# Two passes of one half instead of one pass of two, and a lighter VectorE queue while weights are converted

## The chip, the cores and the metric

The kernel runs on one core of one Trainium2 chip. A core has five engines that work side by side, each from its own queue in a fixed order: TensorE (PE in the profile, with its weight loads as PEld), VectorE (DVE), ScalarE (ACT), GpSimd (POOL) and SyncE (SP), which here issues the transfers. They wait for one another by semaphores. The metric is the device time of one execution in microseconds. The kernel before ran three times: 958.40, 961.85 and 962.46 us, median 961.85.

## The reference

Three blocks, one after the other, all in float32 (the weights of the second come as float64):

- **Attention.** 4 batches, 8 heads, 768 positions, head width 64. A position sees itself and the 127 before it, and the first 4 positions ("sinks"). `a = softmax(q k^T / 8 + mask)`, `out = a v`.
- **MoE.** The attention's output as 3072 tokens of 512 numbers: `y = (sigmoid(x Wg) * (x Wv)) Wo` with 1536 inner columns.
- **Soft MoE.** `logits = y phi` with 32 slots; a softmax over all tokens gathers slots, 8 experts of two layers each work on them, and a softmax over slots spreads the result back over the tokens.

## The kernel before

The tokens fall into 8 **halves** of 384 (batch x half of the sequence). Attention is done half by half: 4 head pairs, each in 3 **units** of 128 queries, so 12 units a half and 96 in all. MoE works on 12 **chunks** of 128 inner columns, each with three weight tiles of 128 x 512 (g, v, o), so 36 tiles. Each number is split into a high and a low part that TensorE multiplies apart (three products instead of one).

**A unit of attention.** `stage_a` multiplies queries and keys (L296), reads the scores out of PSUM with the mask added into `P` (L300, VectorE), and, as the mask leaves at most one of two overlapping key blocks alive in each column, merges the two blocks to 128 columns by a minimum (L306, VectorE); ScalarE takes the exponential of 4 sink columns and 128 others (L312), and one step later `norm` divides by the sum (L316 and L317 on VectorE, L318 on GpSimd). `stage_b` transposes the 128 columns on TensorE (L344) and takes the two key blocks apart again with a triangular mask, twice over 256 columns (L355, VectorE). `stage_c` multiplies by the values (L370).

**A tile of weights.** In its first use a tile comes as float64 bits. `w_start` issues ScalarE's absolute value of the high words (L480); then, one step per call of `w_advance`, `s1` clamps and shifts (L483, L484, VectorE), `s2` puts the sign back (L487) and scales the low words (L488), both VectorE, `s3` adds the two (L491, GpSimd), and `s4` writes the float32 tile to a scratch in DRAM and splits it: the high part on ScalarE (L190), the low part on GpSimd (L462). In every later pass over the weights a tile is loaded from the scratch and only split again (`w_parts`).

**Passes.** `passes` groups the halves: (0,1), (2,3), (4,5), (6,7). A pass goes once over all 12 chunks, and a split tile is used for both halves of the pass; there is room for four chunks of split tiles (`slot`), and a tile of chunk n waits until chunk n-4 is done with (`before`). A step of two chunks and one half is four `gemm1` operations (L595, with the gate's product on VectorE at L606, its high part on ScalarE at L190, later VectorE at L192, and its low part on GpSimd at L608) and three `gemm2` operations (L630, summed on VectorE at L635). The tables `w_due` and `due` say at which operation a tile or a half is needed; `LA` is how many operations ahead a tile may be started, and the loop spreads the attention's pieces up to the due times. Before that loop, a first one does the attention of half 0 alone. An L608 is done once per chunk and half, so 24 of them make a pass of two halves and 96 the MoE. The framework then lists the instructions of each engine in an order that it works out itself, so the order in the code isn't that of the queues.

Of the kernel before, what the change touches and what calls it, by code (L numbers as in the profile page):

```python
# [9 lines left out]
F32 = mybir.dt.float32  # L10
F32R = mybir.dt.float32r
I32 = mybir.dt.int32
BF16 = mybir.dt.bfloat16
U32 = mybir.dt.uint32
# [22 lines left out]
def fused_kernel(ctx, tc, qT, kA, kB, vB, vS, wg, wv, wo, phi, w1, w2, n_sink, window, out):  # L37
# [10 lines left out]
    def ps(tag, bufs, dt=F32):  # L48
        return psum.tile([128, 512], dt, name=tag, tag=tag, bufs=bufs)
# [224 lines left out]
    def stage_a(u):  # L274
        n, jj = units[u]
        hf, p = pairs[n]
        if jj == 0:
            b, s = divmod(hf, 2)
            if s == 0 and p == 0:
                sinks(b)  # L280
            VT[n] = at.tile([128, 4, 128], F32, name="vt", tag="vt", bufs=2)
            sp.dma_start(out=VT[n][:, 0:3 + s], in_=vB[b, p, :, 2 * s:3 + 3 * s])
            while any(t[0] == n for t in at_tasks):
                run_split()
            load_pair(n + 2)
            queue_split(n + 1)
            PC[n] = at.tile([128, 3, 2, 132], F32, name="PC", tag="PC", bufs=2)
        j = 3 * (hf % 2) + jj
        w0, w, mt, blks, sk = UNITS[j]
        P = at.tile([128, 2, 260], F32, name="P", tag="P", bufs=3)  # L290
        nb = at.tile([128, 2], F32, name="nb", tag="nb", bufs=4)
        sm = at.tile([128, 2], F32, name="sm", tag="sm", bufs=4)
        Ss = [ps("ys", 3) for h in range(2)]
        for i, k in enumerate(QK[n][1:]):
            for h in range(2):
                pe.matmul(Ss[h][:, 0:w], QK[n][0][h][:, 128 * jj:128 * jj + 128], k[h][:, w0:w0 + w],  # L296
                          start=(i == 0), stop=(i == len(QK[n]) - 2))
        for h in range(2):
            S = Ss[h]
            dve.tensor_tensor_reduce(  # L300
                out=P[:, h, 0:w], in0=S[:, 0:w], in1=mask[:, MOFF[mt]:MOFF[mt] + w], scale=-0.125,
                scalar=3.0e38, op0=ALU.add, op1=ALU.min, accum_out=nb[:, h:h + 1])

        if sk is not None:
            c0 = sk + 4 if sk else 4
            dve.tensor_tensor(P[:, :, c0:c0 + 128], P[:, :, blks[0][1]:blks[0][1] + 128],  # L306
                              P[:, :, blks[1][1]:blks[1][1] + 128], op=ALU.min)
            src, dst = P[:, :, sk:sk + 132], PC[n][:, jj]
        else:
            src, dst = P[:, :, 0:128], PC[n][:, jj, :, 4:132]  # L310
        for h in range(2):
            act.activation(out=dst[:, h], in_=src[:, h], func=ACTF.Exp, scale=-1.0,  # L312
                           bias=nb[:, h:h + 1], accum_out=sm[:, h:h + 1])

        def norm():
            dve.tensor_scalar(sm, sm, 1.0e-9, None, op0=ALU.add)  # L316
            dve.reciprocal(sm, sm)  # L317
            pool.tensor_tensor(dst, dst, sm.unsqueeze(2).to_broadcast([128, 2, src.shape[2]]), op=ALU.mult)  # L318
            normed.add(u)
            if jj == 2:  # L320
                later(1, sink_parts)

        def sink_parts():
            T, u0 = T2[n % 2], 1 - hf % 2
            cb = PC[n].rearrange("p u h c -> p (u h) c")[:, 2 * u0:6, 0:4]
            cb = cb.unsqueeze(2).to_broadcast([128, 6 - 2 * u0, 2, 4])
            hi, lo = (T[:, 2 * u0:6, :, i] for i in range(2))
            dve.tensor_copy(hi, cb)
            dve.tensor_tensor(lo, cb, hi.bitcast(F32), op=ALU.subtract)
            sunk.add(n)  # L330
        later(1, norm)

    PC, normed, sunk = {}, set(), set()

    def stage_b(u):
        n, jj = units[u]
        hf, p = pairs[n]
        j = 3 * (hf % 2) + jj
        sk = UNITS[j][4]
        while u not in normed or jj == 2 and n not in sunk:  # L340
            tick()
        pt = ps("pt", 1)
        for h in range(2):
            pe.transpose(pt[:, 128 * h:128 * h + 128], PC[n][:, jj, h, 4:132], ident)  # L344
        if jj == 2:
            T, tt = T2[n % 2], tt2[n % 2]
            pe.transpose(pt[:, 256:384].bitcast(F32R), T.rearrange("p u a x s -> p (u a x s)"), identr)
        pts = at.tile([128, 2, 2, 128], F32, name="pts", tag="pts", bufs=4)
        st[u] = pts
        pv = pt[:, 0:256].rearrange("p (h q) -> p h q", h=2)  # L350
        if sk is None:
            act.copy(pts[:, 0], pv)
        else:
            for i in range(2):
                dve.tensor_tensor(pts[:, i], pv, tri[:, i].unsqueeze(1).to_broadcast([128, 2, 128]), op=ALU.mult)  # L355
        if jj == 2:
            for i in range(1 - hf % 2, 3):
                act.copy(tt[32 * i:32 * i + 32, 128 * i:128 * i + 128], pt[32 * i:32 * i + 32, 256:384])

    def stage_c(n):  # L360

# [45 lines left out]
        return True  # L407


    passes = [[h, h + 1] for h in range(0, NH, 2)]  # L410
    W64 = wg.dtype == mybir.dt.int64
    dram = ctx.enter_context(tc.tile_pool(name="dram", bufs=1, space=bass.MemoryType.DRAM))
    wscr = {kd: dram.tile([NF, 128, 512], F32, name="ws" + kd) for kd in "gvo"} if W64 else None
# [53 lines left out]
    def w_start():  # L467
        n, kind = wtiles[ws_n[0]]
        r = w_raw.pop((n, kind))
        ws_n[0] += 1  # L470
        if not (n < NF and W64):
            w_parts(n, kind, r)
            w_load()
            return


        L, H = r[:, :, 0], r[:, :, 1]
        A = tops[0].tile([128, 512], I32, name="wA", tag="wA", bufs=3)
        S = tops[0].tile([128, 512], I32, name="wS", tag="wS", bufs=2)
        act.activation(out=A.bitcast(F32), in_=H.bitcast(F32), func=ACTF.Abs)  # L480

        def s1():
            dve.tensor_scalar(A.bitcast(F32), A.bitcast(F32), F64_LO, F64_HI, op0=ALU.max, op1=ALU.min)  # L483
            dve.tensor_scalar(A, A, 3, 0x3FFFFFF8, op0=ALU.logical_shift_left, op1=ALU.bitwise_and)  # L484

        def s2():
            dve.scalar_tensor_tensor(A, H, -0x40000000, A, op0=ALU.bitwise_and, op1=ALU.bitwise_or)  # L487
            dve.tensor_scalar(S, L.bitcast(U32), 2.0 ** -29, None, op0=ALU.mult)  # L488

        def s3():  # L490
            pool.tensor_tensor(A, A, S, op=ALU.add)  # L491
            w_load()

        def s4():
            sp.dma_start(out=wscr[kind][chunks[n]], in_=A.bitcast(F32))
            w_parts(n, kind, A.bitcast(F32))
        w_fly[n, kind] = deque([s1, s2, s3, s4])
# [15 lines left out]

    def w_slot():
        w_advance()
        if w_can(LA) and len(w_fly) < 3:
            w_start()

    xs = {}
# [455 lines left out]
    while done_half[0] < 1:  # L975
        attn_piece()
        tick()
        w_slot()
    while w_can(0) or w_fly:
        w_slot()  # L980
    fast = nc.values_load(flag, min_val=0, max_val=1)
    phase[0] = 0

# [114 lines left out]
```

## Time and profile before

| | |
|---|---|
| three runs | 958.40, 961.85, 962.46 us |
| the profiled execution | 956.84 us, its span 955.0 us |
| busy over the span | PE 903.7, PEld 739.1, DVE 650.8, POOL 477.5, ACT 351.0 us |
| last weight tile converted (36th L491) | ends at 270.2 us |
| 24th, 48th, 72nd and 96th L608 | end at 327.3, 524.6, 718.9 and 879.3 us |

Busy time is the time in which an engine works on instructions; a wait inside an instruction counts as busy. PEclk is TensorE's granted clock as a share of 2.4 GHz. The idle time of an engine that nothing waits for costs nothing, so the stretches have to be read one by one.

### The profile page before, as it was taken

What the parts mean: (1) busy time and instruction counts of PE and PEld (TensorE: products, weight loads), DVE (VectorE), ACT (ScalarE), POOL (GpSimd) and SP (SyncE); (2) the same over time, 40 slices, a digit from 0 to 9 for tenths busy, and PEclk for the clock granted to TensorE, in tenths of its full rate; (3) what the DMA queues carried; (4) which work ended last, traced back from release to release, by engine and by line L of the source; (5) the groups of instructions that cost most, each with busy time, mean ns of one, the idle gap of its engine ahead of it and who ended that gap; (6) DMA issues with size and microseconds to landing.
All of it is one profiled execution on the core that took longest, in us unless ns stands there. A gap on an engine that the chain in (4) does not pass through costs nothing.

```text
span 955.0 us, 15394 instructions
## 1 busy us (share of the span) xinstructions
PE 903.7 (95%) x5369; PEld 739.1 (77%) x5369; DVE 650.8 (68%) x1633; ACT 351.0 (37%) x957; POOL 477.5 (50%) x437
## 2 busy tenths in 40 slices
PE   8787998989889999999999999999999999999894
PEld 3444767768678878999999889999988899998443
DVE  8999567899986656677687866667754454546522
ACT  3443336444443433434334445333333322222221
POOL 3665316666665344766756647666432364553000
PEclk7555899999999999999999999999999999999897
DMA  6665212564322131433332224332147632324999
GB/s 222 217 188 171 94 56 86 171 198 161 115 84 81 31 86 52 104 99 97 91 81 78 79 64 114 97 86 79 45 165 260 243 94 66 79 77 143 316 352 306
DMA packets 75605, 124.83 MB, mean 131 GB/s; under 512 B 6272, under 2 KB 37888, under 8 KB 75520
## 3 DMA queue, kind: packets, MB, share of 16 engines
q1 hardware_dynamic: 75520, 123.77, 42.6%
q8 instruction: 44, 0.72, 0.3%
q14 instruction: 41, 0.34, 0.1%
HBM read 108.02 MB, written 15.73 MB: 130 GB/s over the span
## 4 chain that ended last, share of the span: by engine, by line
PE 76%; DVE 14%; issue 3%; DMA 2%; POOL 2%; ACT 1%; SPq 1%; DVEq 0%; ACTq 0%
PE gv L595 38%; PE ys L630 19%; PE ys L296 5%; PE xt L370 4%; DVE wA L484 2%; PE pt L344 2%; DVE wA L483 2%; PE ys L812 2%; DVE wA L487 2%; DVE wS L488 1%; DVE P L300 1%; DVE sm L316 1%; PE ys L657 1%; DMA wbits<-in_wg_dram 1%; PE ys L666 1%
## 5 line engine op out<-in xcount | busy, mean ns | idle before, releaser
L608 POOL TENSOR_TENSOR gl<-th,gh 128x384 fp32r<-128x384 f32 x96 | 101.6, 1058 | 154.3 <-DVE gh L192 117.0
L595 PE MATMUL gv<-xh,whg 128*128 128x384 f32 x384 | 135.1, 352 | 0.0
L595 PE MATMUL gv<-xh,whv 128*128 128x384 f32 x384 | 133.9, 349 | 0.0
L595 PE MATMUL gv<-xl,whg 128*128 128x384 f32 x384 | 132.3, 344 | 0.0
L595 PE MATMUL gv<-xh,wlg 128*128 128x384 f32 x384 | 132.3, 344 | 0.0
L595 PE MATMUL gv<-xh,wlv 128*128 128x384 f32 x384 | 131.8, 343 | 0.0
L595 PE MATMUL gv<-xl,whv 128*128 128x384 f32 x384 | 131.3, 342 | 0.0
L312 ACT ACTIVATE PC<-P,nb 128x132 f32<-128x132 f32 (+1 forms) x192 | 75.9, 396 | 149.4 <-DVE P L306 102.3
L630 PE MATMUL ys<-who,gh 128*128 128x512 f32 x288 | 118.7, 412 | 10.4 <-DVE ysb L635 8.6
L635 DVE SCALAR_TENSOR_TENSOR ysb<-ys,ysb 128x512 f32<-128x512 f32 x156 | 105.2, 682 | 33.7 <-PE ys L630 33.3
L630 PE MATMUL ys<-who,gl 128*128 128x512 f32 x288 | 114.3, 397 | 0.0
L630 PE MATMUL ys<-wlo,gh 128*128 128x512 f32 x288 | 114.2, 397 | 0.0
L318 POOL TENSOR_TENSOR PC<-PC,sm 128x264 f32<-128x264 f32 (+1 forms) x96 | 62.9, 657 | 98.7 <-DVE sm L317 61.5
L606 DVE SCALAR_TENSOR_TENSOR th<-th,gv 128x384 f32<-128x384 f32 x96 | 52.8, 550 | 84.1 <-PE gv L595 77.0
L300 DVE CUSTOM_DVE_ANT_0 P<-ys,mask 128x260 f32<-128x260 f32 (+1 forms) x192 | 72.7, 396 | 17.3 <-PE ys L296 17.1
L296 PE MATMUL ys<-rk,rq 64*128 64x260 f32 (+1 forms) x204 | 67.0, 502 | 17.8 <-DVE nb L300 16.3
L595 PEld LDWEIGHTS gv<-xh,whg 128*128 128x128 f32 x384 | 73.5, 191 | 5.8 <-issue 3.7
L595 PEld LDWEIGHTS gv<-xh,whv 128*128 128x128 f32 x384 | 73.5, 191 | 4.9 <-issue 3.4
L595 PEld LDWEIGHTS gv<-xl,whg 128*128 128x128 f32 x384 | 73.5, 191 | 4.5 <-issue 1.9
L630 PEld LDWEIGHTS ys<-who,gh 128*128 128x128 f32 x288 | 54.2, 188 | 29.1 <-DVE ysb L635 10.2
L595 PEld LDWEIGHTS gv<-xh,wlv 128*128 128x128 f32 x384 | 73.2, 191 | 3.1 <-issue 1.7
L595 PEld LDWEIGHTS gv<-xl,whv 128*128 128x128 f32 x384 | 73.4, 191 | 2.4 <-issue 0.7
(199 smaller groups left out, 1787.9 us busy)
## 6 DMA issues: line engine op xcount, KB each, us to landing
ew<-in_w_dram SPq DMA_DIRECT2D x32, 1024.0 KB, 11.6
wraw<-wsg SPq DMA_DIRECT2D x38, 256.0 KB, 2.7
wraw<-wsv SPq DMA_DIRECT2D x38, 256.0 KB, 2.7
wraw<-wso SPq DMA_DIRECT2D x38, 256.0 KB, 2.7
wbits<-in_wg_dram SPq DMA_DIRECT2D x12, 512.0 KB, 4.7
wbits<-in_wv_dram SPq DMA_DIRECT2D x12, 512.0 KB, 3.7
wbits<-in_wo_dram SPq DMA_DIRECT2D x12, 512.0 KB, 3.5
out_dram<-ew SPq DMA_DIRECT2D x8, 768.0 KB, 8.8
```

The costliest lines, as they stand in the source:

```text
L296: pe.matmul(Ss[h][:, 0:w], QK[n][0][h][:, 128 * jj:128 * jj + 128], k[h][:, w0:w0 + w], start=(i == 0), stop=(i == len(QK[n]) - 2))
L300: dve.tensor_tensor_reduce(out=P[:, h, 0:w], in0=S[:, 0:w], in1=mask[:, MOFF[mt]:MOFF[mt] + w], scale=-0.125, scalar=3.0e38, op0=ALU.add, ...
L312: act.activation(out=dst[:, h], in_=src[:, h], func=ACTF.Exp, scale=-1.0, bias=nb[:, h:h + 1], accum_out=sm[:, h:h + 1])
L318: pool.tensor_tensor(dst, dst, sm.unsqueeze(2).to_broadcast([128, 2, src.shape[2]]), op=ALU.mult)
L344: pe.transpose(pt[:, 128 * h:128 * h + 128], PC[n][:, jj, h, 4:132], ident)
L370: pe.matmul(xt[64 * h:64 * h + 64, cols], VT[n][:, jj + s - i, 64 * h:64 * h + 64], pts[:, i, h, :], start=(jj == 0 and i == 0), stop=Fals ...
L483: dve.tensor_scalar(A.bitcast(F32), A.bitcast(F32), F64_LO, F64_HI, op0=ALU.max, op1=ALU.min)
L595: pe.matmul(acc_ps[:, 0:384], wt[:, 128 * d:128 * d + 128], xt[:, d, :], start=(k == 0), stop=(k == 11))
L606: dve.scalar_tensor_tensor(gr, th, 1.0, acc_ps[:, 0:384], op0=ALU.add, op1=ALU.mult)
L608: pool.tensor_tensor(gl, gr, gh.bitcast(F32), op=ALU.subtract)
L630: pe.matmul(yp, a[:, 128 * i:128 * i + 128], w, start=(k == 0), stop=(k == 3 * len(ns) - 1))
L635: dve.scalar_tensor_tensor(ysb[h][:, i, :], yp, 0.5, ysb[h][:, i, :], op0=ALU.mult, op1=ALU.add)
```

## The change

There are four edits.

1. **Passes.** `passes` becomes (0), (1), (2,3), (4,5), (6,7): halves 0 and 1 go over the 12 chunks one after the other. Half 1 is needed later, and there are five passes over the weights instead of four.
2. **Low words.** L488 moves from VectorE to ScalarE, and from `s2` into `w_start`.
3. **Wide units.** While the conversion's memory is there (`len(tops) == 1`) and for units of the first two halves (u < 24) that have two key blocks (`sk is not None`; 20 units), the blocks aren't merged: no L306 and no L355, but the exponential, the sum's division and the copy out of PSUM go over both blocks (260 columns per head, 512 transposed columns), four transposes instead of two, and a copy of the 4 sink columns on ScalarE behind the division.
4. **Starts.** `w_slot` may start a tile 8 operations ahead instead of 4 until all are started, and the loop that finished the conversions in flight before the MoE goes.

```diff
+        wide = sk is not None and u < 24 and len(tops) == 1
+        if wide:
+            P = tops[0].tile([128, 2, 260], F32, name="PW", tag="PW", bufs=4)
+        else:
+            P = at.tile([128, 2, 260], F32, name="P", tag="P", bufs=3)
...
+        if wide:
+            src = dst = P
+            PW[u] = P
+            wides.add(u)
+        elif sk is not None:
             c0 = sk + 4 if sk else 4
             dve.tensor_tensor(P[:, :, c0:c0 + 128], P[:, :, blks[0][1]:blks[0][1] + 128],
...
             pool.tensor_tensor(dst, dst, sm.unsqueeze(2).to_broadcast([128, 2, src.shape[2]]), op=ALU.mult)
+            if wide:
+                act.copy(PC[n][:, jj, :, 0:4], P[:, :, sk:sk + 4])
...
+        if u in PW:
+            P = PW.pop(u)
+            for i, (_, off) in enumerate(reversed(UNITS[j][3])):
+                for h in range(2):
+                    pe.transpose(pt[:, 256 * i + 128 * h:256 * i + 128 * h + 128], P[:, h, off:off + 128], ident)
+            act.copy(pts.rearrange("p i h q -> p (i h q)"), pt)
+            if jj == 2:
+                tT = ps("xt", 1)
...
-    passes = [[h, h + 1] for h in range(0, NH, 2)]
+    passes = [[0], [1]] + [[h, h + 1] for h in range(2, NH, 2)]
...
         act.activation(out=A.bitcast(F32), in_=H.bitcast(F32), func=ACTF.Abs)
+        act.mul(S, L.bitcast(U32), 2.0 ** -29)
...
-            dve.tensor_scalar(S, L.bitcast(U32), 2.0 ** -29, None, op0=ALU.mult)
...
-        if w_can(LA) and len(w_fly) < 3:
+        if w_can(LA if ws_n[0] >= 3 * NF else 2 * LA) and len(w_fly) < 3:
...
-        w_slot()
-    while w_can(0) or w_fly:
-        w_slot()
+        if ws_n[0] < 6 or w_fly:
+            w_slot()
```

GpSimd's queue shortly before the last conversion. `wA<-wA,wS` is a conversion's addition, `wlg`, `wlv` and `wlo` are low parts of tiles (from `wA` in their first pass, from `wraw` when loaded again), `gl` is the low part of a gate's product, `PC` the division of a narrow unit. Before:

```order
L491 TENSOR_TENSOR wA<-wA,wS 128x512
L318 TENSOR_TENSOR PC<-PC,sm 128x264
L462 TENSOR_TENSOR wlg<-wA,whg 128x512
L608 TENSOR_TENSOR gl<-th,gh 128x384
L491 TENSOR_TENSOR wA<-wA,wS 128x512
L462 TENSOR_TENSOR wlv<-wA,whv 128x512
L608 TENSOR_TENSOR gl<-th,gh 128x384
L318 TENSOR_TENSOR PC<-PC,sm 128x264
L462 TENSOR_TENSOR wlo<-wA,who 128x512 x2
L491 TENSOR_TENSOR wA<-wA,wS 128x512 x2
L608 TENSOR_TENSOR gl<-th,gh 128x384
```

And of the changed kernel, whose lines 514, 485, 631 and 327 are the same four:

```order
L514 TENSOR_TENSOR wA<-wA,wS 128x512
L485 TENSOR_TENSOR wlv<-wA,whv 128x512
L514 TENSOR_TENSOR wA<-wA,wS 128x512
L327 TENSOR_TENSOR PC<-PC,sm 128x264
L485 TENSOR_TENSOR wlo<-wA,who 128x512
L485 TENSOR_TENSOR wlg<-wraw,whg 128x512
L485 TENSOR_TENSOR wlo<-wraw,who 128x512 x2
L485 TENSOR_TENSOR wlg<-wA,whg 128x512
L514 TENSOR_TENSOR wA<-wA,wS 128x512
L327 TENSOR_TENSOR PC<-PC,sm 128x2x128
L631 TENSOR_TENSOR gl<-th,gh 128x384
```

Between the conversions there are now low parts of tiles that are loaded a second time for half 1, and fewer gate products. Up to the 36th addition, GpSimd's queue held 18 `gl`, 34 low parts and 41 divisions before; it holds 11 `gl`, 41 low parts and 31 divisions now, 20 of these over 520 columns.

ScalarE's queue in the attention of half 0, before (`tta` is the transposed sink part, `whv`, `who` and `whg` are high parts):

```order
L480 ACTIVATE wA<-wbits 128x512
L190 CAST whv<-wA 128x512
L312 ACTIVATE PC,sm<-P,nb 128x128 x2
L312 ACTIVATE PC,sm<-P,nb 128x132 x2
L480 ACTIVATE wA<-wbits 128x512
L358 CAST tta<-pt 32x128 x2
L312 ACTIVATE PC,sm<-P,nb 128x132 x2
```

And of the changed kernel, in the same place (L503 is L480, L504 scales the low words, L321 is L312, L329 copies the sink columns, L362 copies a wide unit's transposed blocks):

```order
L190 CAST whg<-wA 128x512
L504 ACTIVATE wS<-wbits 128x512
L329 COPY PC<-PW 128x2x4
L503 ACTIVATE wA<-wbits 128x512
L362 COPY pts<-pt 128x512
L190 CAST whv<-wA 128x512
L504 ACTIVATE wS<-wbits 128x512
L321 ACTIVATE PC,sm<-P,nb 128x128 x2
L321 ACTIVATE PW,sm<-PW,nb 128x260 x2
L374 COPY pts<-pt 128x256
L329 COPY PC<-PW 128x2x4
```

The scaling and the two copies have come in, and the copy of the sink columns, which waits for GpSimd's division, stands ahead of the conversion's first steps of later tiles.

## Rows read from the trace of the kernel before

**Rows 1.** Busy us by stretch; columns named in the first row.

```profile
core 0: us, PE busy (x) PEld busy (x) DVE busy (x) ACT busy (x) POOL busy (x), PEclk, DMA share, GB/s
32.90:105.30 72.40, 60.61 (x225) 36.72 (x222) 66.35 (x177) 29.78 (x92) 39.82 (x36) 0.58 0.55 178
105.30:167.50 62.20, 59.28 (x343) 44.12 (x343) 40.97 (x125) 27.54 (x86) 23.64 (x25) 0.97 0.26 78
167.50:270.20 102.70, 94.63 (x531) 76.69 (x531) 95.41 (x202) 45.30 (x116) 68.10 (x59) 1.00 0.48 155
270.20:327.30 57.10, 53.47 (x311) 43.18 (x312) 38.24 (x91) 23.93 (x67) 29.01 (x28) 0.97 0.26 72
327.30:524.60 197.30, 197.30 (x1219) 174.07 (x1218) 136.82 (x351) 77.61 (x220) 117.32 (x106) 1.00 0.31 83
```

**Rows 2.** Timeline of GpSimd: start us, duration us, engine, line, operation, tiles.

```profile
31.45 1.45 POOL L491 TENSOR_TENSOR wA<-wA,wS 128x512 int32<-128x512 int32 x1
...
103.99 1.28 POOL L491 TENSOR_TENSOR wA<-wA,wS 128x512 int32<-128x512 int32 x1 [3.01 <-DVE sm L316]
...
165.99 1.47 POOL L491 TENSOR_TENSOR wA<-wA,wS 128x512 int32<-128x512 int32 x1 [1.23 <-DVE wA L487]
...
268.92 1.28 POOL L491 TENSOR_TENSOR wA<-wA,wS 128x512 int32<-128x512 int32 x1
...
326.31 1.01 POOL L608 TENSOR_TENSOR gl<-th,gh 128x384 fp32r<-128x384 f32 x1 [3.12 <-ACT gh L190]
...
523.33 1.25 POOL L608 TENSOR_TENSOR gl<-th,gh 128x384 fp32r<-128x384 f32 x1 [4.60 <-DVE gh L192]
...
717.73 1.17 POOL L608 TENSOR_TENSOR gl<-th,gh 128x384 fp32r<-128x384 f32 x1 [8.95 <-DVE gh L192]
...
878.30 1.01 POOL L608 TENSOR_TENSOR gl<-th,gh 128x384 fp32r<-128x384 f32 x1 [2.52 <-DVE gh L192]
```

**Rows 3.** By line, to 270.2 us, VectorE: ns min/median/max, first and last start.

```profile
L483 DVE TENSOR_SCALAR wA<-wA x36: 398/418/1509, 13.3 to 264.9; 128x512 f32<-128x512 f32 x36
L484 DVE TENSOR_SCALAR wA<-wA x36: 410/426/1517, 15.7 to 265.4; 128x512 int32<-128x512 int32 x36
L487 DVE SCALAR_TENSOR_TENSOR wA<-wbits,wA x36: 676/688/1665, 18.2 to 266.2; 128x512 int32<-128x512 int32 x36
L488 DVE TENSOR_SCALAR wS<-wbits x36: 399/552/1511, 12.1 to 260.7; 128x512 int32<-128x512 uint32 x36
L306 DVE TENSOR_TENSOR P<-P x34: 398/414/1483, 11.1 to 264.1; 128x256 f32<-128x256 f32 x34
L316 DVE TENSOR_SCALAR sm<-sm x42: 139/169/1254, 10.5 to 266.8; 128x2 f32<-128x2 f32 x42
L536 DVE TENSOR_TENSOR xl<-xraw,xh x8: 542/550/979, 44.3 to 148.5; 128x384 fp32r<-128x384 f32 x8
```

**Rows 4.** The same for two VectorE lines that read PSUM.

```profile
L300 DVE CUSTOM_DVE_ANT_0 P<-ys,mask x84: 264/415/429, 8.7 to 263.6; 128x260 f32<-128x260 f32 x68, 128x128 f32<-128x128 f32 x16
L355 DVE TENSOR_TENSOR pts<-pt,tri x64: 396/414/425, 22.6 to 270.1; 128x256 f32<-128x256 f32 x64
```

**Rows 5.** Timeline, 19 to 21 us.

```profile
18.97 1.38 POOL L491 TENSOR_TENSOR wA<-wA,wS 128x512 int32<-128x512 int32 x1 [1.72 <-DVE wA L487]
19.15 1.48 DVE L306 TENSOR_TENSOR P<-P 128x256 f32<-128x256 f32 x1
```

**Rows 6.** By line, to 270.2 us, GpSimd: ns min/median/max.

```profile
L491 POOL TENSOR_TENSOR wA<-wA,wS x36: 1264/1293/1652, 19.0 to 268.9; 128x512 int32<-128x512 int32 x36
L462 POOL TENSOR_TENSOR wlv<-wA,whv x12: 1261/1414/1527, 26.8 to 266.5; 128x512 fp32r<-128x512 f32 x12
L608 POOL TENSOR_TENSOR gl<-th,gh x18: 992/1057/1300, 100.0 to 267.9; 128x384 fp32r<-128x384 f32 x18
L318 POOL TENSOR_TENSOR PC<-PC,sm x42: 612/627/1074, 11.7 to 270.2; 128x264 f32<-128x264 f32 x34, 128x256 f32<-128x256 f32 x8
```

**Rows 7.** The same for ScalarE's first step of the conversion.

```profile
L480 ACT ACTIVATE wA<-wbits x36: 647/673/698, 12.1 to 262.4; 128x512 f32<-128x512 f32 x36
```

More of the change, by code (lines that the diff above doesn't have):

```diff
@@ L289, in stage_a @@
         w0, w, mt, blks, sk = UNITS[j]
-        P = at.tile([128, 2, 260], F32, name="P", tag="P", bufs=3)
+        wide = sk is not None and u < 24 and len(tops) == 1
[3 more added lines that the diff above has]
+            P = at.tile([128, 2, 260], F32, name="P", tag="P", bufs=3)
         nb = at.tile([128, 2], F32, name="nb", tag="nb", bufs=4)
@@ L302, in stage_a @@
                 scalar=3.0e38, op0=ALU.add, op1=ALU.min, accum_out=nb[:, h:h + 1])
-        if sk is not None:
+        if wide:
[3 more added lines that the diff above has]
+        elif sk is not None:
             c0 = sk + 4 if sk else 4
@@ L331, in stage_a @@
         later(1, norm)
-    PC, normed, sunk = {}, set(), set()
+    PC, PW, wides, normed, sunk = {}, {}, set(), set(), set()
     def stage_b(u):
@@ L342, in stage_b @@
         pt = ps("pt", 1)
-        for h in range(2):
-            pe.transpose(pt[:, 128 * h:128 * h + 128], PC[n][:, jj, h, 4:132], ident)
+        pts = at.tile([128, 2, 2, 128], F32, name="pts", tag="pts", bufs=4)
+        st[u] = pts
+        tT = None
+        if u in PW:
[6 more added lines that the diff above has]
+                tT = ps("xt", 1)
+        else:
+            for h in range(2):
+                pe.transpose(pt[:, 128 * h:128 * h + 128], PC[n][:, jj, h, 4:132], ident)
         if jj == 2:
             T, tt = T2[n % 2], tt2[n % 2]
-            pe.transpose(pt[:, 256:384].bitcast(F32R), T.rearrange("p u a x s -> p (u a x s)"), identr)
-        pts = at.tile([128, 2, 2, 128], F32, name="pts", tag="pts", bufs=4)
-        st[u] = pts
+            tT = (pt if tT is None else tT)[:, 256:384]
+            pe.transpose(tT.bitcast(F32R), T.rearrange("p u a x s -> p (u a x s)"), identr)
         pv = pt[:, 0:256].rearrange("p (h q) -> p h q", h=2)
-        if sk is None:
+        if u not in wides and sk is None:
             act.copy(pts[:, 0], pv)
-        else:
+        elif u not in wides:
             for i in range(2):
@@ L357, in stage_b @@
             for i in range(1 - hf % 2, 3):
-                act.copy(tt[32 * i:32 * i + 32, 128 * i:128 * i + 128], pt[32 * i:32 * i + 32, 256:384])
+                act.copy(tt[32 * i:32 * i + 32, 128 * i:128 * i + 128], tT[32 * i:32 * i + 32])
     def stage_c(n):
```

## The prediction

> **What bounds the kernel now.** I read the busy time by stretch first, cut at four additions of the conversion (the 3rd, 15th, 18th and 36th L491) and at the end of the first pass (the 24th L608) [rows 1, 2]. From 327.3 us on TensorE is busy without a break at a granted clock of 1.00 (2.4 GHz): 24 chunk products and 24 attention units take 524.6 - 327.3 = 197.3 us. Before that it isn't: in 32.9 to 105.3 us it stands at 0.58 of its clock, and VectorE is busy 66.4 of 72.4 us; in 167.5 to 270.2 us VectorE is busy 95.4 of 102.7 us. In between, from 105.3 to 167.5 us, only three tiles are converted and VectorE has 21 us free.
>
> Then I read what VectorE's busy time is made of. The conversion's own lines and the merge take 0.40, 0.41, 0.68, 0.40 and 0.40 us at the shortest and up to 1.67 us at the longest [rows 3]. The two lines that read PSUM don't stretch: 264 to 429 and 396 to 425 ns [rows 4]. One pair shows why: a merge starts at 19.15 us, 0.18 us after a GpSimd addition, and ends at 20.63, 0.28 us after that addition's end at 20.35, so it lasts 1.48 us where 0.40 suffice [rows 5]. So these VectorE lines and GpSimd's lines take turns. I count both together as "the port": L483, L484, L487, L488, L306, L316 and L536 on VectorE, all of GpSimd.
>
> By the Trainium skill (SBUF — State Buffer, Who interferes with whom) a VectorE instruction with two SBUF inputs, or in a two-port mode, and a GpSimd instruction block each other for a whole instruction; the rows agree, 1.48 us against 0.40. It speaks against this change, which takes work off VectorE and gives GpSimd more. By that rule the sum is the one below; without it, it would be that of the third rival.
>
> Is the port full? Shortest durations [rows 3, 6] times the counts of each queue between the marks:
> - 32.9 to 105.3 us: GpSimd 12 additions x 1.26 + 10 low parts x 1.26 + 12 divisions x 0.61 + 1 gate part x 0.99 = 36.0; VectorE 12 tiles x (0.40 + 0.41 + 0.68 + 0.40 = 1.88) + 13 merges x 0.40 + 12 sums x 0.14 + 4 splits x 0.54 = 31.6. Together 67.6 of 72.4 us.
> - 167.5 to 270.2 us: 18 x 1.26 + 18 x 1.26 + 11 x 0.99 + 11 x 0.61 = 63.0; 18 x 1.88 less one L488 + 10 x 0.40 + 11 x 0.14 = 39.0. Together 102 of 102.7 us.
> - 105.3 to 167.5 us: 22.1 + 12.7 = 35 of 62.2 us.
>
> So 97% in the two dense stretches, and 56% between them. The conversion is bound by the port, the rest by TensorE.
>
> **The change part by part.**
>
> *Low words to ScalarE.* 36 x 0.40 = 14.4 us leave the port. ScalarE gets 36 instructions; its nearest row, L480 with the same shape and input, takes 0.67 us [rows 7], so 24 us, beside an engine that is busy 103 of the 237 us to 270.2 [rows 1]. It hides, as long as ScalarE's queue doesn't stand.
>
> *Wide units.* 20 merges go, 20 x 0.40 = 8 us of port; 40 x 0.41 = 16.6 us of L355 go from VectorE, but not from the port. The division over 520 instead of 264 columns is bounded below by the narrow one, 0.61 us, and above by the addition over 512 columns with two full inputs, 1.26 us [rows 6]. I take the narrow one in proportion, 0.61 x 520 / 264 = 1.21 us: 20 x 0.59 = 12 us more of port. So this edit gives the port nothing back (between -8 and +5 us). It adds 40 transposes and the longer exponentials and copies on TensorE and ScalarE, neither full here. It adds a wait too: the sink copy on ScalarE waits for the division on GpSimd, and behind it in that queue stand the absolute value and the scaling of later tiles, for which VectorE and then GpSimd wait. I give that no price of its own; it is why I don't count on a full port below.
>
> *Starts.* Eight operations ahead instead of four costs no instruction; what it moves is in the counts of the new queues below.
>
> *Passes.* 36 tiles are loaded and split once more: 36 x 1.26 = 45.4 us more of GpSimd and port, 36 high parts on ScalarE, 9.4 MB more of DMA while the queues were used 26 to 55% [rows 1]. And only half as much MoE stands beside the conversion: by the new queues' counts, at the 36th addition 11 chunk products and 31 units are done, before 18 and 41.
>
> *The sum, to the last conversion.* From the 3rd to the 36th addition the new queues hold: GpSimd 33 x 1.26 + 40 low parts x 1.26 + 11 x 0.99 + 9 x 0.61 + 16 wide x 1.21 = 127.8 (118 with the lower bound of the wide one); VectorE 33 x 1.48 + 5 x 0.40 + 25 x 0.14 + 8 x 0.54 = 58.8. Together 186.6 us. The 3rd addition I set at 32 us (32.9 before). At the 97% of the dense stretches the last conversion ends at 32 + 192 = 224 us. I take 93%, as a thinner VectorE queue waits more often for others than one that was never idle: 201 us, so 233 us; it was 270.2.
>
> *From there to the state of before at 327.3 us* (24 chunk products, 48 units). A chunk product alone costs (879.3 - 718.9) / 24 = 6.68 us [rows 2]; then a unit with its share of the soft MoE costs (197.3 - 24 x 6.68) / 24 = 1.54 us. Missing are 13 and 17: 13 x 6.68 + 17 x 1.54 = 113 us, if TensorE is busy throughout. Before, 270.2 to 327.3 us lost 57.1 - (6 x 6.68 + 7 x 1.54) = 6 us, where the conversion's memory is handed over; I keep them. So 233 + 119 = 352 us, where before had 327.3: 25 us later. What remains, 72 chunk products and 48 units in three passes, is the same. In short, the conversion ends 37 us earlier with 7 products and 10 units less done, which are 62 us.
>
> The profiled execution took 956.84 us for a span of 955.0; with 25 more, 982. It lay 5 us under the median of the three runs, so **987 us**.
>
> **The rivals.**
> - *TensorE's clock stays low while tiles are converted.* In 32.9 to 105.3 us it was 0.58, and with less MoE beside the conversion TensorE has more gaps; against it, from 167.5 us on it was 1.00 although tiles were converted. At 1.2 GHz the 11 products and 25 units after 32 us cost twice as much: 2 x (11 x 6.68 + 25 x 1.54) = 224 us, so the conversion ends at 256 and the state is reached at 375 us, +48: 1010 us.
> - *It comes out even.* If the instructions overlap at their ends (TensorE's idle 6 us go too) and the port works off 100% of the shortest durations, 32 + 187 + 113 = 332 us, +5, and with the wide division at its lower bound 322 us, -5: 957 to 967 us.
> - *Faster: VectorE's queue was the limit, not the port.* For it: VectorE's 92 to 93%, and its 14 + 8 + 17 us that go. If VectorE's thinner queue slips under GpSimd's instructions without cost, GpSimd alone decides, 127.8 us at 95%: the last conversion at 167 us, the state at 286, -41; halfway between that and the port's 224 us, at 195 us, the state is reached at 314, -13. So 921 to 949, 935 us in the middle. It gains from where the last conversion ends before 327 - 119 = 208 us. Against it: the stretched rows.
>
> That the change doesn't do what it says is out: the queues show the wide divisions, the second low parts and the scaling on ScalarE.
>
> **How the numbers follow.** The forecast (the port at 97 down to 88%, the last conversion at 224 to 244 us, so 978 to 998 us) gets 0.58, the low clock 0.15, even 0.11, faster 0.16. A measurement of this kernel can't tell 0.5%, some 5 us, from no change. Slower are the first two and 0.03 of the third, 0.76; within 0.5% the other 0.08; faster 0.16. The range leaves out the stronger half of the faster case and the worst of the low clock: 948 to 1018 us.
>
> **What would show it.** Right: the 36th addition at 224 to 245 us with 11 gate parts before it; the 24th L608's successor (L631) at 340 to 365 us; the merge, clamps and shifts that remain stretched to over 1 us beside GpSimd; GpSimd busy some 65% up to the last conversion, against 55 and 66% in the dense stretches before; the same 197 us per pass after that. Wrong: the 36th addition before 208 us, or the 24th gate part before 327 us. A clock under 0.8 between 105 us and the last conversion would speak for the low clock.

## The result, and the profile after

The changed kernel takes **950.1 us** (949.3 to 950.9, 4 runs) against 960.3 (958.4 to 962.5, 4 runs) before: ratio 0.989 [0.987, 0.992], so 1.1% faster. The prediction said 987 us and slower, in a range of 948 to 1018. The time lies just inside that range, but the sign is wrong.

The profiled execution took 949.64 us for a span of 947.9. Busy time by stretch, cut at the same events as [rows 1] (3rd, 15th, 18th and 36th addition, 24th and 48th gate part; the columns are those of [rows 1]):

```profile
30.20:94.10 63.90, 54.53 (x291) 40.63 (x291) 52.67 (x114) 47.60 (x126) 47.52 (x41) 0.75 0.63 199
94.10:109.00 14.90, 14.70 (x85) 11.14 (x85) 9.41 (x25) 11.50 (x30) 10.39 (x10) 1.00 0.50 159
109.00:204.10 95.10, 83.56 (x401) 62.85 (x400) 91.23 (x176) 60.02 (x148) 79.55 (x63) 0.82 0.58 182
204.10:318.40 114.30, 114.30 (x663) 93.69 (x663) 81.44 (x200) 51.77 (x140) 84.35 (x74) 1.00 0.42 117
318.40:516.70 198.30, 197.14 (x1233) 175.76 (x1232) 145.36 (x361) 82.92 (x235) 132.29 (x118) 1.00 0.36 96
```

The conversion no longer pauses between the 15th and the 18th tile (14.9 us, before 62.2), TensorE has no gap after the last conversion (114.30 of 114.30 us), and from the 24th gate part on nothing has changed (198.3 us to the 48th, before 197.3). GpSimd's timeline gives the marks that answer to [rows 2] (start and duration in us; the 3rd, 15th and 36th addition, the 24th and 48th gate part):

```profile
28.77 1.44 POOL L514 TENSOR_TENSOR wA<-wA,wS 128x512 int32<-128x512 int32 x1
...
92.81 1.29 POOL L514 TENSOR_TENSOR wA<-wA,wS 128x512 int32<-128x512 int32 x1 [0.69 <-POOL wlv L485]
...
202.86 1.28 POOL L514 TENSOR_TENSOR wA<-wA,wS 128x512 int32<-128x512 int32 x1 [1.70 <-PE xt L392]
...
317.40 1.02 POOL L631 TENSOR_TENSOR gl<-th,gh 128x384 fp32r<-128x384 f32 x1 [0.83 <-PE ys L653]
...
515.45 1.25 POOL L631 TENSOR_TENSOR gl<-th,gh 128x384 fp32r<-128x384 f32 x1 [5.09 <-DVE gh L192]
```

So the last conversion ends at 204.1 us (before 270.2, predicted 233) and the 24th gate part at 318.4 (before 327.3, predicted 352). At the 36th addition 11 gate parts and 31 units are done, as the queues said. Durations by line (ns, shortest/median/longest), the answers to [rows 3, 6 and 7]: the clamp is still stretched, the wide division takes 1.05 us at the shortest, the scaling on ScalarE 0.67.

```profile
L507 DVE TENSOR_SCALAR wA<-wA x36: 408/835/1545, 12.9 to 198.9; 128x512 f32<-128x512 f32 x36
L511 DVE SCALAR_TENSOR_TENSOR wA<-wbits,wA x36: 667/691/1786, 16.9 to 202.0; 128x512 int32<-128x512 int32 x36
L327 POOL TENSOR_TENSOR PW<-PW,sm x20: 1046/1076/1502, 13.1 to 137.5; 128x520 f32<-128x520 f32 x20
L504 ACT ACTIVATE wS<-wbits x36: 647/668/705, 12.3 to 193.6; 128x512 int32<-128x512 uint32 x36
```

### The profile page after: what moved, and what is told of

The parts are those of the page before. It is cut to its first block, busy times and chain, and to the rows that moved or that the text cites. A ratio compares the mean times of both kernels' runs of the same rounds, so it can differ in the third digit from the quotient of the medians.

```text
span 947.9 us, 15728 instructions
## 1 busy us (share of the span) xinstructions
PE 902.1 (95%) x5408; PEld 748.0 (79%) x5409; DVE 648.7 (68%) x1553; ACT 403.9 (43%) x1061; POOL 553.8 (58%) x485
## 4 chain that ended last, share of the span: by engine, by line
## 5 line engine op out<-in xcount | busy, mean ns | idle before, releaser
L618 PE MATMUL gv<-xh,wlg 128*128 128x384 f32 x384 | 134.3, 350 | 0.0
L321 ACT ACTIVATE PC<-P,nb 128x132 f32<-128x132 f32 (+1 forms) x152 | 60.3, 397 | 125.6 <-DVE P L315 92.5
L485 POOL TENSOR_TENSOR wlg<-wraw,whg 128x512 fp32r<-128x512 f32 x50 | 66.8, 1336 | 35.6 <-ACT whg L190 33.1
L485 POOL TENSOR_TENSOR wlv<-wraw,whv 128x512 fp32r<-128x512 f32 x50 | 65.8, 1316 | 29.6 <-ACT whv L190 29.5
L327 POOL TENSOR_TENSOR PC<-PC,sm 128x264 f32<-128x264 f32 (+1 forms) x76 | 50.8, 669 | 51.1 <-DVE sm L326 38.4
L618 PEld LDWEIGHTS gv<-xh,wlg 128*128 128x128 f32 x384 | 74.8, 195 | 4.2 <-issue 2.9
```

Of the source, the lines that this page charges most:

```text
L485: pool.tensor_tensor(lo, r, hi.bitcast(F32), op=ALU.subtract)
L618: pe.matmul(acc_ps[:, 0:384], wt[:, 128 * d:128 * d + 128], xt[:, d, :], start=(k == 0), stop=(k == 11))
```

## The experiments

All kernels but the first are the kernel before or the changed one with one thing altered. Times are medians, ratios are to runs of the kernel before on the same chip (in brackets the 95% interval); the last two columns are the ends of the 36th addition and the 24th gate part in the profiled execution.

| kernel | us | ratio [95%] | 36th | 24th |
|---|---|---|---|---|
| before | 960.3 | | 270.2 | 327.3 |
| changed | 950.1 | 0.989 [0.987, 0.992] | 204.1 | 318.4 |
| before + passes (e_passes) | 963.4 | 1.003 [1.001, 1.004] | 223.3 | 334.8 |
| before + scaling (e_scale) | 950.8 | 0.989 [0.987, 0.991] | 261.8 | 321.4 |
| before + wide (e_wide) | 947.1 | 0.986 [0.982, 0.989] | 258.0 | 316.4 |
| before + scaling + wide (e_pairs) | 939.8 | 0.978 [0.976, 0.980] | 250.0 | 309.8 |
| changed, old starts (e_nostart) | 949.3 | 0.988 [0.984, 0.991] | 206.2 | 319.2 |
| before + 36 GpSimd additions (p_pool_b) | 954.8 | 0.994 [0.992, 0.996] | 278.6 | 325.6 |
| before + 36 tensor_scalars (p_ts_b) | 963.6 | 1.003 [1.001, 1.004] | 278.1 | 338.2 |
| before + 36 maxima (p_red_b) | 954.2 | 0.993 [0.991, 0.996] | 265.9 | 325.8 |
| changed + 36 GpSimd additions (p_pool_a) | 979.0 | 1.018 [1.014, 1.021] | 245.4 | 351.8 |
| changed + 36 tensor_scalars (p_ts_a) | 962.5 | 1.002 [1.000, 1.003] | 222.8 | 331.9 |
| changed + 36 maxima (p_red_a) | 952.2 | 0.990 [0.987, 0.993] | 214.5 | 325.6 |
| before, no merges (x_nomerge) | 953.9 | 0.993 [0.991, 0.996] | 266.0 | 323.1 |
| before, no products (x_nomask) | 946.4 | 0.984 [0.981, 0.987] | 261.0 | 318.5 |
| the same + 40 maxima (x_nomask_red) | 951.9 | 0.991 [0.988, 0.995] | 264.5 | 321.9 |
| e_pairs, no 1e-9 (g_noadd) | 938.7 | 0.977 [0.975, 0.980] | 249.7 | 308.7 |
| g_noadd, wide division on ScalarE (g_actdiv) | 937.9 | 0.977 [0.974, 0.980] | 246.8 | 304.3 |
| changed, no 1e-9, that division (a_actdiv) | 934.9 | 0.974 [0.970, 0.978] | 196.8 | 305.6 |

From the 24th gate part to the end of the span there are 625 to 630 us in every row, so the question is only what comes before it.

**What a pair costs.** Streams of 40 instructions of each kind, alone and beside a stream of GpSimd subtractions; nothing of the reference is computed:

```diff
+    for f in (TS, TT, PT, RD, AC):   # clamp, merge, product out of PSUM, maximum, ScalarE copy
+        barrier()
+        for _ in range(40):
+            P()                      # GpSimd subtraction, 128x512
+            f()
```

> Measures the disputed price by itself; it computes nothing of the reference and writes zeros. 40 GpSimd subtractions of 128x512 (the low part's shape) alone; 40 of each of four VectorE forms alone (clamp 128x512, merge 128x256, product of PSUM and SBUF 128x256, maximum over 384 of one SBUF input); then 40 GpSimd subtractions beside 40 of each, beside 40 ScalarE copies, and beside 80 clamps. If the two engines take turns for the whole of their shortest durations, a pair of subtraction and clamp takes 1.26 + 0.40 = 1.66 us, a pair with a merge the same, and with the PSUM product or the maximum 1.26. If the port is held for less than the durations that a trace shows, the clamp and the merge pairs take less, 1.3 to 1.55 us, by which my sum of shortest durations was too long.

By line and stretch (ns shortest/median/longest): GpSimd alone, VectorE alone, both, and GpSimd beside the product out of PSUM:

```profile
L38 POOL TENSOR_TENSOR po<-pa,pb x40: 1261/1262/1262, 11.9 to 64.1; 128x512 f32<-128x512 f32 x40
...
L39 DVE TENSOR_SCALAR do<-da x40: 426/427/428, 66.0 to 84.0; 128x512 f32<-128x512 f32 x40
...
L38 POOL TENSOR_TENSOR po<-pa,pb x40: 1320/1322/1323, 146.4 to 201.0; 128x512 f32<-128x512 f32 x40
L39 DVE TENSOR_SCALAR do<-da x40: 426/1366/1369, 146.2 to 199.9; 128x512 f32<-128x512 f32 x40
...
L38 POOL TENSOR_TENSOR po<-pa,pb x40: 1262/1262/1267, 259.9 to 312.3; 128x512 f32<-128x512 f32 x40
L41 DVE TENSOR_TENSOR do<-x,db x40: 423/424/425, 259.7 to 277.6; 128x256 f32<-128x256 f32 x40
```

From first start to last, 39 subtractions take (64.1 - 11.9) / 39 = 1.34 us each alone and (201.0 - 146.4) / 39 = 1.40 beside the clamps: GpSimd pays 0.06 us, and VectorE waits, one clamp for each subtraction. A pair costs 1.40 us and not 1.26 + 0.40 = 1.66, which the prediction's sum charges. The product out of PSUM costs GpSimd nothing (1262 ns, as alone) and isn't stretched itself.

**The edits one by one.** The diffs are those of the change.

> The kernel before with the passes alone changed; low words stay on VectorE, no wide units, starts as before. Port theory (GpSimd and the VectorE lines with two SBUF inputs or a two-port mode take turns and bind the conversion, but hold the port shorter than I summed): the port's work from the 3rd to the 36th addition is 12 + 6 us more than in the changed kernel, less 9 us of wide divisions, so the last conversion ends some 10 us after the changed kernel's 204, at 212 to 218 us, and the run takes 956 to 965 us. Queue theory (VectorE's queue, its own work plus its waits, binds): VectorE has 13 + 7 + 17 us more of its own, the last conversion ends at 230 us or later and the run takes 970 to 980 us.

> The kernel before with the scaling of the low words on ScalarE alone. Port theory: 0.40 us less of port for the 29 tiles in the two dense stretches, 12 us: 946 to 952 us. Queue theory: L488 goes with its waits, 12 x 0.70 + 17 x 0.91 = 24 us: 934 to 942 us. If the stretch between the dense ones or TensorE takes it back: 957 to 960 us.

> The changed kernel with the passes and the starts of before: scaling on ScalarE and wide units, but pairs of halves. Port theory: 12 us less for the scaling, 8 less for the merges, 9 more for the wide divisions, so 944 to 952 us, no slower than the changed kernel. Queue theory: 24 us of the scaling, 13 of the merges and 17 of the triangles go from VectorE, where it binds: 920 to 935 us. If the passes are what gains, it stays at 957 to 962 us.

> The kernel before with the wide units alone. The prediction gave this edit between -8 and +5 us of port and counted the 16.6 us of the product out of PSUM for nothing. Port: within 5 us of 960. If VectorE's own time counts beside GpSimd's, 8 + 17 us of VectorE go: 5 to 12 us faster, 948 to 955. Beside the scaling on ScalarE the same edit was worth 11 us.

> The changed kernel without the fourth edit (tiles may start 4 operations ahead again, and the loop that finishes the conversions in flight before the MoE is back). If the earlier starts fill GpSimd and VectorE from 100 to 200 us, the last conversion ends later without them, at 215 to 235 us, and the time is 5 to 15 us above the changed kernel's 950. If they do nothing, the last conversion stays at 204 and the time at 950.

The passes alone cost 0.3%; the scaling alone gives 1.1%, the wide units alone 1.4%, both 2.2%. The starts do nothing. The changed kernel is 10 us slower than scaling and wide units without the other two edits. So the passes are a loss here, a small one, and the whole gain comes from the two edits that lighten VectorE. The wide units, to which the prediction gave nothing, give at least as much as the scaling. Of the expectations, the scaling came out as the port theory had it (946 to 952 us); the 36th addition of the passes alone (223.3 us) and the time of the two edits together (939.8) fell between the two theories.

**Is the port full?** One useless instruction per converted tile, behind the store of the tile, first in the kernel before and then in the changed one:

```diff
             sp.dma_start(out=wscr[kind][chunks[n]], in_=A.bitcast(F32))
+            pool.tensor_tensor(scr, A.bitcast(F32), A.bitcast(F32), op=ALU.add)             # p_pool
+            dve.tensor_scalar(scr, A.bitcast(F32), 2.0, None, op0=ALU.mult)                 # p_ts
+            dve.tensor_reduce(scr[:, 0:1], A.bitcast(F32)[:, 0:256], axis=AX.X, op=ALU.max) # p_red
```

> The kernel before, with one VectorE instruction more for each of the 36 converted tiles: a maximum over 256 columns of the finished tile, one SBUF input, which didn't stretch beside GpSimd when measured alone; its result is not used. Slot theory (beside a busy GpSimd VectorE gets one sharing instruction in per GpSimd instruction and hardly slows GpSimd, so that VectorE's queue, its own work plus its waits, binds the dense stretches): 29 tiles fall into the dense stretches, each costs its own 0.42 us, 12 us: 970 to 975 us. Port theory (turns on the port bind, VectorE's other work is free beside them): 958 to 963 us.

> The kernel before with one VectorE instruction more for each converted tile of the same 0.42 us, but one that shares with GpSimd: the finished tile times 2 over 512 columns, not used. Slot theory: its own 0.42 us and a wait like that of L488 (0.30 to 0.50 us on the mean) for 29 tiles, so 20 to 27 us: 978 to 988 us, clearly more than the maximum costs. Port theory: 29 x 0.40 = 12 us: 970 to 974 us. Were VectorE's queue alone the limit and waits nothing: the same as the maximum.

> The kernel before with one GpSimd instruction more for each converted tile, the finished tile added to itself (128x512, 1.26 us), not used. Port theory: 29 x 1.26 = 37 us in the dense stretches: 990 to 998 us. Slot theory: GpSimd has 45 and 34% of the dense stretches free, so it costs only what VectorE's instructions wait longer, at 0.63 us per us of GpSimd (72 us of both busy to 108 us of GpSimd there) 23 us at the most, and less where it falls beside VectorE's PSUM lines: 968 to 985 us.

In the kernel before, 45 us of GpSimd work and 15 us of VectorE work that doesn't share the port don't show in the time; both kernels are even 6 us faster. All three expectations missed, under either theory. By stretch the additions do show. With them the conversion needs 89.6 us from the 3rd to the 15th tile (before 72.4) and 113.5 from the 18th to the 36th (102.7), and the pause between, 39.5 us instead of 62.2, takes most of that back:

```profile
36.00:125.60 89.60, 79.31 (x366) 53.36 (x367) 86.59 (x229) 38.10 (x116) 61.00 (x57) 0.75 0.46 153
165.10:278.60 113.50, 101.58 (x545) 82.44 (x542) 107.05 (x206) 45.40 (x117) 88.93 (x77) 0.95 0.40 138
```

Still, these stretches had room before. The first of them now also holds 6 more divisions and 3 more gate parts. Counted as in the prediction, with GpSimd at 34 x 1.26 + 18 x 0.61 + 4 x 0.99 = 57.8 and 54 x 1.26 + 11 x 0.61 + 11 x 0.99 = 85.6 us, they hold 57.8 + 34.6 = 92.4 us of shortest durations in 89.6, and 85.6 + 39.4 = 125 in 113.5: 103 and 110%, where it was 93 and 99%. Neither the port nor VectorE's time was full there over the whole conversion.

As these edits only add work, a difference of 6 us between two of these kernels can come from the new order that the framework gives the queues; single differences below that are not read further. The traces show that the order changes: in the kernel before, GpSimd's queue departs from the old one at its 21st instruction with the additions and at its 23rd with the maxima. So the unchanged time is that of the added work and the new order together. The kernels with maxima and with tensor_scalars, however, have the same order on VectorE, ScalarE and GpSimd up to the 24th gate part, before and after the change. The tensor_scalar costs 9 us more than the maximum, and this difference is that of the instruction.

> The changed kernel with one more GpSimd addition (128x512, result unused) per converted tile, 36 in all, 48 us of GpSimd at the measured pace of 1.34 us. Port full (the prediction's view): the last conversion ends 36 x 1.26 = 45 us later, at 249 us, and most of it shows in the time, 20 to 45 us. Pairs slip in (a VectorE instruction fits beside a GpSimd one for 0.06 us): the added additions also carry VectorE instructions that would have needed room of their own, so 36 x (1.40 - 0.42) = 35 us later at most and 0.2 x that less where GpSimd has gaps (it was busy 80% of the stretch): 20 to 35 us, 10 to 30 us in the time. VectorE's queue decides: last conversion within 10 us, time within 5 us of the changed kernel's.

> The changed kernel with one more VectorE tensor_scalar (128x512 from and to SBUF, result unused) per converted tile, 36 in all. It puts back the kind of work that the scaling on ScalarE took away. Port full: 36 x 0.41 = 15 us later to the last conversion, at 219 us, and 6 to 15 us in the time. Pairs slip in: the stretch has more VectorE instructions of this kind (137) than GpSimd instructions (109), so each added one needs 0.4 us of its own or a stretched 0.8: 15 to 30 us later, 6 to 20 in the time. Neither decides: within 3 us.

> The changed kernel with one more VectorE maximum over 256 columns per converted tile, 36 in all, about 0.4 us each and 15 us together; by the separate measurement it doesn't share the port. Port: last conversion within 3 us of 204 and time within 3 us of 950, while the same time as a tensor_scalar moved the last conversion by 19 us and the time by 12. VectorE's queue: last conversion 10 to 15 us later.

In the changed kernel it is different. GpSimd's timeline with the additions shows the 36th conversion and the 24th gate part:

```profile
244.09 1.29 POOL L515 TENSOR_TENSOR wA<-wA,wS 128x512 int32<-128x512 int32 x1 [0.98 <-DVE wA L512]
...
350.78 1.01 POOL L633 TENSOR_TENSOR gl<-th,gh 128x384 fp32r<-128x384 f32 x1
```

From the 3rd to the 36th addition there are 213.9 us instead of 173.9: 40.0 us for 33 tiles, 1.21 us each, which is what the added instruction itself takes (median 1214 ns). That is its full duration, as on a resource that is full (the order changes here, too, but 29 us of time are far more than the 6 above). The tensor_scalar adds 191.0 - 173.9 = 17.1 us there, 0.52 each, and the maximum 9.7 us, 0.29 each. These two take the same time on VectorE where nothing stretches them (0.41 and 0.40 us) and stand in the same order (ns shortest/median/longest). The tensor_scalar in p_ts_a:

```profile
L520 DVE TENSOR_SCALAR scr<-wA x36: 410/1180/1539, 24.5 to 224.1; 128x512 f32<-128x512 f32 x36
```

and the maximum in p_red_a:

```profile
L520 DVE TENSOR_REDUCE scr<-wA x36: 400/407/421, 23.6 to 215.7; 128x1 f32<-128x256 f32 x36
```

In the time the three cost 29, 12 and 2 us. The expectation for the maximum held in the time but not in its profiled execution (36th addition 10 us later), which was the slowest of its four (949.1 to 954.3). Whether VectorE's time by itself counts a little in the changed kernel stays open; that GpSimd's does, and the sharing with GpSimd, is shown.

**What the wide units save.** In the kernel before, for the same 20 units, the merge left out or the two products out of PSUM replaced by ScalarE copies (so the second key block's weights, or the masks between the blocks, are missing); then the same VectorE time put back where nothing waits for it:

```diff
-                dve.tensor_tensor(pts[:, i], pv, tri[:, i].unsqueeze(1).to_broadcast([128, 2, 128]), op=ALU.mult)
+                if u in wides:
+                    act.copy(pts[:, i], pv)                          # x_nomask
+                    dve.tensor_reduce(scr[:, i:i + 1], pts[:, i]...) # x_nomask_red only
```

> The kernel before without the 20 merges of the units that become wide (the second key block's scores aren't merged in, so its weights are left out). 20 x 0.40 = 8 us leave VectorE and the port. If only work on the port counts and the stretch is full: up to 8 us faster. As the merges lie mostly before 150 us, where the conversion waits for free slots, 0 to 3 us by the same view. If the unit's path through VectorE counts: 3 to 8 us.

> The kernel before, where for the 20 units that become wide the two triangular products out of PSUM are plain copies on ScalarE (the mask is left out, so the two key blocks aren't kept apart). 40 x 0.41 = 16.6 us leave VectorE that the prediction counted for nothing, since they don't share the port. If VectorE's own time or a unit's path through it is what the wide units save: 5 to 14 us faster than before, the 24th gate part at 313 to 322 us. If only work on the port counts: 24th gate part within 3 us of before's 327.

> The kernel of the run before with the triangular products left out (946.4 us), and behind each of its 40 copies a VectorE maximum over the same 256 columns, about 0.42 us, whose result nothing waits for. VectorE's time is that of the kernel before again, the unit's path stays without VectorE. If VectorE's time counts: the gain of 15 us is gone, 957 to 962 us, 24th gate part at 325 to 329 us. If the place in the unit's path counts: within 4 us of 946, 24th gate part at 316 to 322 us.

The 40 products, 16.6 us that don't touch the port, are worth 15 us: as much as the wide units altogether. The merges are worth 7, close to what the order alone can do. With 40 maxima of 405 ns in the queue again, 5 of the 15 us go and 9 stay. This would say that the larger part isn't VectorE's time but the place of the product: between the transposes on TensorE and the product with the values, in a queue whose other instructions are stretched by GpSimd. It isn't shown: the queues are reordered between these kernels, too, and the waits in that place are short. To 270 us TensorE stands idle before the product with the values for 4.8 us (9 times) until L355 has written, and for 2.2 us (4 times) until the copies have; 2.6 us less is not 15.

A rival that none of these runs separates is TensorE's granted clock. From 80 to 105 us (columns as in [rows 1]; before, then without the products):

```profile
80.00:105.00 25.00, 20.94 (x86) 14.70 (x87) 19.72 (x57) 9.75 (x34) 11.47 (x11) 0.65 0.46 153
80.00:105.00 25.00, 23.63 (x142) 17.82 (x143) 23.86 (x62) 14.78 (x49) 15.98 (x16) 1.00 0.53 171
```

Without the products TensorE runs 142 instructions there instead of 86, at 2.4 GHz throughout. Over the whole run, (1 - granted clock) x time is the time by which the clock fell short of full. By the medians of the runs it is 12 to 13 us less than before with the wide units (of 14 us gained) and without the products (of 15), 8 with the maxima back (of 9), and 6 with the useless maxima or additions in the kernel before (of 6 to 7), but only 2 with the scaling (of 10) and without the merges (of 7); with the useless tensor_scalars it is 3 us less, and the kernel is 3 us slower. So the wide units may gain through an earlier full clock, the scaling hardly. Whether the clock is the cause or follows from a TensorE that waits less stays open.

**Faster versions.** The 1e-9 added to the sum is left out in all three, and in two of them the wide division goes to ScalarE:

```diff
-            pool.tensor_tensor(dst, dst, sm.unsqueeze(2).to_broadcast([128, 2, src.shape[2]]), op=ALU.mult)
+            if wide:
+                for h in range(2):
+                    act.activation(out=dst[:, h], in_=dst[:, h], func=ACTF.Copy, scale=sm[:, h:h + 1])
+            else:
+                pool.tensor_tensor(dst, dst, sm.unsqueeze(2).to_broadcast([128, 2, src.shape[2]]), op=ALU.mult)
```

> The changed kernel with the passes and starts of before, and without the addition of 1e-9 to the softmax's sums (L316), which changes no bit as each sum holds an exponential of 0, so is at least 1. The instruction works 0.14 us, but took 0.44 us on the mean of the 42 before 280 us in the kernel before, as it shares with GpSimd. Slot theory: 26 of them in the dense stretches at 0.49 us, 12 us: 925 to 931 us. Port theory: 26 x 0.14 = 4 us: 934 to 938 us.

> The 939.8 us version (scaling on ScalarE and wide units, passes of two halves) without the 1e-9 added to the sum, and with the wide units' division on ScalarE instead of GpSimd. 20 x 1.05 = 21 us leave GpSimd, ScalarE gets 40 instructions over 260 columns. In passes of two halves added GpSimd work cost nothing, so removed work should bring nothing either: within 3 us of 939. If GpSimd's time counts here as in the changed kernel: 5 to 15 us faster.

> The changed kernel (five passes) with the wide units' division on ScalarE instead of GpSimd, and without the 1e-9 added to the sum. About 16 x 1.05 = 17 us leave GpSimd between the 3rd and the 36th addition. In passes of two halves this brought nothing. If in the passes of one half the port sets the pace, as the added GpSimd and tensor_scalar instructions say: last conversion at 187 to 194 us instead of 204, the time 6 to 14 us under 950. If it doesn't: last conversion within 4 us of 204.

With passes of two halves the 21 us taken off GpSimd bring 1 us, less than the measurement tells from nothing; in the changed kernel they bring 15 us (with the 1e-9, which brought 1), from 950.1 to 934.9, the fastest version here. But the expectation of a faster pace fell: from the 3rd to the 36th addition there are still 171.9 us (173.9). It is faster only to the 15th (51.0 us, in the changed kernel 63.9); from there to the 18th it takes 22.7 instead of 14.9 and to the 36th 98.2 instead of 95.1. The 3rd comes 5.3 us earlier, and from the 36th to the 24th gate part it is 108.8 us instead of 114.3. The busy time by stretch (columns as in [rows 1]; to the 15th, to the 36th addition):

```profile
24.90:75.90 51.00, 39.35 (x190) 26.36 (x187) 41.13 (x91) 47.44 (x132) 32.52 (x26) 0.69 0.75 244
75.90:196.80 120.90, 106.32 (x606) 82.90 (x607) 98.59 (x199) 84.96 (x214) 87.33 (x70) 0.96 0.51 172
```

ScalarE is busy 47.4 of the first 51.0 us, the highest of the four, while GpSimd has fallen to 64%. So ScalarE may be what is late next; no run shows it.

With passes of two halves the same gain goes into the pause: g_actdiv needs 51.8 us to the 15th addition (e_pairs 65.7), and then pauses 71.5 us to the 18th (59.3).

## Why the prediction was wrong, step by step

- **Where the change acts: right.** Everything is decided before the 24th gate part.
- **From the last conversion to that state: right but for the stall.** 113 us of TensorE's work were predicted, and 6 us lost at the handover; it took 114.3, without a gap.
- **The last conversion at 233 us, "at the 97% of the dense stretches" or, as taken, 93%: wrong.** This step holds 29 of the 37 us of error. It came at 204.1: the sum of 186.6 us was done in 173.9, 107%. With the wide division at its measured 1.05 instead of 1.21 us the sum is 184.0, still 106%. What failed is the reading of a sum of shortest durations as a ceiling, which made the port's work too long. By the separate measurement a subtraction with one VectorE instruction beside it costs 1.40 us and not 1.66. If each of the 33 additions and 40 low parts has such a partner, 73 x 0.26 = 19 us go, and 186.6 - 19 = 168 us are 96% of 173.9. By the same price the dense stretches before were (67.6 - 22 x 0.26) / 72.4 = 85% and (102 - 36 x 0.26) / 102.7 = 90% full. So two things were off together: the port's price was too high, and what looked like a full port before was one with room, as the additions show (103 and 110% of the same stretches by the same count). The split between the two is arithmetic, not shown by a run.
- **That the port sets the pace of the conversion: half right for the changed kernel, wrong for the one before as a whole.** After the change each added GpSimd instruction costs its whole duration; but 16 wide divisions taken off GpSimd between the 3rd and the 36th addition shorten that stretch by only 2.0 us (a_actdiv), so the port doesn't set it alone. Before the change, the dense stretches took 17 and 11 us longer with the additions, and the pause between the 15th and the 18th tile took 23 of these 28 us back. The prediction took the pace from a kernel that was waiting for other things part of the time. The rule of the Trainium skill that it quoted (SBUF — State Buffer, Who interferes with whom), by which one of the two blocks while the other holds the port, holds here for VectorE (0.43 us become 1.37) but not for GpSimd (1.26 become 1.32). By the pair as measured, the sum charged for both what, to 0.06 us, only one of them pays.
- **The wide units at nothing: wrong.** "L355 go from VectorE, not from the port" was true and beside the point: taking those products out of VectorE's queue is worth 15 us in passes of two halves, the new order of the queues included. The prediction looked for one bound and charged only what touched it. By which way the 15 us come, the place in VectorE's queue or TensorE's clock, stays open.
- **The passes as a large loss: right in sign, too large.** By the prediction 7 products and 10 units less at the last conversion (62 us) stood against an earlier end of it, 37 us with all edits together. With the passes alone the last conversion ends 47 us earlier than before (223.3) and the 24th gate part 7.5 later; on top of the other edits the passes cost 10 us.
- **The scaling on ScalarE at 0.67 us, hidden: right.** 0.668 us; alone it gives 10 us.
- **The base: 4.5 us.** The profiled execution of before lay 5 us under the median of the three runs (3.4 under that of the four); that of the changed kernel only 0.5 under its own.
- **The rivals.** Gains were to start where the last conversion ends before 208 us; it ended at 204. So the third rival's sign came true just beyond its weak end (950.1 us, it said 921 to 949), but its mechanism only by half: VectorE does slip in beside GpSimd, yet not without cost, as the tensor_scalars show. The clock from 109 to 204 us was 0.82 (before, from 105.3 to 167.5 us 0.97 and then 1.00), but from 30.2 to 94.1 us it was 0.75, and 0.58 before; over the whole run it fell short by 10 us less, so the low clock didn't come true as a loss.

Of the error of 37 us, 29 are the pace of the conversion, 5 the stall, 4.5 the base, and 1.7 go the other way in the rest.

## What to carry to other kernels

An engine or a port that is busy 97% by a sum of durations isn't shown to be the limit: add a useless instruction per step to it, and see whether its duration comes back in the time. Look stretch by stretch, as a pause elsewhere can swallow it, and compare two useless instructions that leave the queues in the same order, of which only one uses the resource. Two instructions that take turns are to be priced as a pair, measured side by side. And work that is taken out of a queue in which others are stretched should be priced by who waits for it, too, and not only by the resource that it uses, though how much of the 15 us that was here no run shows.

## What the runs showed of the hardware

- GpSimd and VectorE on SBUF don't share evenly: with both streams waiting, GpSimd keeps 1.40 us per subtraction (alone 1.34) and VectorE gets one clamp in that time instead of one per 0.46 us. With two clamps per subtraction, half of the 80 clamps ran only when the subtractions were done, in 19 us from 479 to 498 us, 0.48 us each.
- A maximum over columns and a product out of PSUM aren't stretched beside GpSimd (407 and 424 ns at the median), a tensor_scalar of the same length is (1180 ns in p_ts_a).
- TensorE's granted clock from 30 to 80 us was 0.53 before and 0.70 with scaling and wide units, where the wide units give TensorE two more transposes each; at 80 us both kernels had finished the division of 15 units. From 80 to 105 us it was 0.65 and 0.81, with 86 and 143 TensorE instructions.
